# Stores issued later, activation tiles loaded two token tiles ahead, and the input layer's maxima replaced by row sums of its squares

## The chip, the core and the metric

The kernel runs on one core of a Trainium2 chip. A core has five engines that work beside each other, each through its own queue in order: TensorE (PE in the profile; PEld is its weight load), VectorE (DVE), ScalarE (ACT), GpSimd (POOL) and SyncE (SP), which here does nothing but issue transfers. Sixteen DMA engines carry the transfers. The metric is the device time of one execution, in microseconds (us), lower is better.

## The reference

Three stages follow each other: an attention whose heads are mixed before and after the softmax, a gated layer, and a layer with a squared ReLU.

```python
scores = scale * q @ k.T ; scores = mix_heads(scores, w_pre)       # 4 x 12 x 448 x 448
attn   = softmax(scores) ; attn   = mix_heads(attn, w_post)
x      = (attn @ v) laid out as 1792 tokens x 768
x      = ((x @ w1) * (x @ w2)) @ w3 @ w_out                        # 768 -> 1024 -> 1024 -> 768
h      = x @ moe2_w_in                                             # 768 -> 2048
g      = max(h, 0) ** 2
out    = g @ moe2_w_out                                            # 2048 -> 768
```

The weights of the two layers arrive as 64-bit floats. The kernel decodes them into 32-bit floats itself, and splits every factor of a product into a high and a low 16-bit half, so that a product costs three matmuls.

## The kernel before, in words

The change touches only the last third of the program, from about 832 us on: the **input layer** (`h` and `g`) and the **output layer** (`g @ moe2_w_out`).

The input layer takes the 2048 columns in eight pairs of blocks of 128 (`layer_in`). One pair is eight calls of `in_tile` (two blocks by four groups of 448 tokens), each 18 matmuls at line 1074, so 144 a pair. `in_tile` evicts a product with a ReLU on ACT (L1560), squares it in place on ACT (L1561), takes the maximum of each row of the product on DVE (`gm`, L1562), and issues a store of the square to a DRAM tensor `g` on SP (L1563). After the fourth and the eighth pair `g_scale` reduces `gm` to one number per partition (`gx`) and `send` carries it through DRAM to all partitions (`across`, then `ac`, L828 and L831, both on POOL's queue). From it comes the power of two by which `g` is scaled into 16 bits.

Beside the matmuls a stream of steps prepares weights: a chunk of 768 KB is loaded on SP into one of two `raw` buffers (L747), decoded by two ACT and four DVE operations (L797 to L811, tiles `zt` and `xa`), and either sent for a common scale and cast (`tot`, `across`, `ac`, `ws`, `w`, L889 and L892: the input weights) or stored as `kept_out` (L967: the output weights). Each raw buffer is loaded again as soon as its decode is over. A second stream, `mixed_out`, loads the kept output weights again (`ob`), adds and subtracts their quarters on POOL (`ot`, L1495) and casts the seven combinations (`ow`, L1527 and L1530): the output layer is done by a scheme that needs seven quarter products in the place of eight.

The output layer takes the tokens in 14 tiles (128 rows of either half), the first seven against the first half of the 2048 columns (partial sums stored to `acc`), the last seven against the second half (`acc` loaded again as `al`, results stored to `out`). One token tile is seven `multiply` calls of 12 matmuls (L1662), 84 in all. For it the stream `mixed_tokens` loads four quarters of `g` (`gt`, 256 KB each, L1586), forms four sums on POOL (L1594, `ss` and `gt`), and casts seven combinations to 16 bits on ACT (high half, L1615) and DVE (low half, L1616) into `ao`. `take` evicts a product: on ACT (L1676) where nothing is added, on DVE (L1678) where something is.

What sets the order: a planner in the program's own text. `now` is a planned clock that `tick` moves on, `busy` a planned load of ACT, DVE and POOL, and each stream emits its next step when its engine's planned load is less than `ahead` us in front of the clock. A transfer is written into SP's queue at the place where the program calls for it; SP then stands until that transfer's source or buffer is ready, and everything behind it stands too.

Of the kernel before, what the change touches and what calls it, by code (L numbers as in the profile page):

```python
# [10 lines left out]
F32 = mybir.dt.float32  # L11
# [7 lines left out]
P = 128  # L19
# [16 lines left out]
def talking_heads_attention_moe_moe2(  # L36
# [749 lines left out]
    def decode(raw, n, total=None, x=None, zt=None):  # L786

        lo, hi = (raw.rearrange("p (f two) -> p f two", two=2)[:, :, w] for w in (0, 1))
        z = hi.bitcast(F32)
        if x is None:  # L790
            x = pools["w"].tile([P, DM], F32, tag="xa", name="xa", bufs=3)[:, :n]
        xi = x.bitcast(I32)
        if zt is None:
            zt = pools["w"].tile([P, DM], F32, tag="zt", name="zt", bufs=1)[:, :n]
        r = n / DM
        return x, [
            (ACT, 0.9 * r, lambda: nc.scalar.activation(zt, z, AF.Abs)),  # L797
            (DVE, 1.0 * r, lambda: nc.vector.tensor_scalar(
                xi, lo, 29, 0x40000000, op0=ALU.logical_shift_right, op1=ALU.bitwise_or
            )),  # L800
            (REST, HAND, None),
            (DVE, 0.6 * r, lambda: nc.vector.tensor_scalar(
                zt, zt, F64_LEAST, F64_MOST, op0=ALU.max, op1=ALU.min
            )),
            (DVE, 1.0 * r, lambda: nc.vector.scalar_tensor_tensor(  # L805
                xi, zt.bitcast(I32), 3, xi, op0=ALU.logical_shift_left, op1=ALU.bitwise_xor
            )),
            (REST, HAND, None),
            (ACT, 1.0 * r, lambda: nc.scalar.activation(x, x, AF.Abs, accum_out=total)),  # L809
            (REST, HAND, None),  # L810
            (DVE, 1.0 * r, lambda: nc.vector.scalar_tensor_tensor(  # L811
                xi, hi, -(2 ** 31), xi, op0=ALU.bitwise_and, op1=ALU.bitwise_or
            )),
        ]
# [3 lines left out]
    def w_tile(ring, name="w"):  # L818
        return pools["w"].tile([P, 2, DM], F16, tag="wv"[ring], name=name, bufs=WB)
# [128 lines left out]
    def one_steps(i):  # L948
        kind, j = chunks[i]
        load_to(i + 1)  # L950
        t = wraw.pop(i)
        if kind == "wl":
            load_to(i + 2)
            hh = wo_tiles(j)[0]
            yield ACT, 0.9, lambda: nc.scalar.copy(hh, t.bitcast(F32))

            def low():
                nc.vector.tensor_tensor(t, t.bitcast(F32), hh, op=ALU.subtract)
                wsp["wo", j] = wsp[chunks[i]] = (hh, t)

            yield DVE, 1.0, low
            return
        n = 4 * P if kind == "w3" else DM
        if kind == "out":
            x, ops = decode(t, n, out_sums[j // OG][:, j % OG : j % OG + 1])
            yield from read_raw(i, x, ops)
            yield POOL, 0, lambda: nc.sync.dma_start(kept_out[j], x)  # L967
            if j % OG == OG - 1:
                streams.append(mixed_out(j // OG))
            return  # L970
        x, ops = (decode_alone if kind == "w3" else decode)(t, n)
        yield from read_raw(i, x, ops)
        if kind == "w3":
            hh, ll = (
                pools["w"].tile([P, 4 * P], F32R, tag="wv"[z], name="w3", bufs=WB) for z in range(2)
            )
        elif j >= NFC // 2:
            yield POOL, 0, lambda: nc.sync.dma_start(kept[j], x)
            return
        else:  # L980
            hh, ll = wo_tiles(j)
        yield ACT, 0.9 * n / DM, lambda: nc.scalar.copy(hh, x)

        def low():
            nc.gpsimd.tensor_tensor(ll, x, hh, op=ALU.subtract)
            wsp[kind, j] = (hh, ll)

        yield POOL, 2.0, low
# [54 lines left out]
    allow, ahead = [1], [4.0]  # L1043
    weights = Stream(weight_steps(2))

    def tick(us, act=0.0, dve=0.0):
        now[0] += us
        for e, c in ((ACT, act), (DVE, dve)):
            busy[e] = max(busy[e], now[0] - us) + c
        for st in streams + [weights]:  # L1050
            r = True
            while r:
                r = st.step()
            if r is None and st in streams:
                streams.remove(st)
# [29 lines left out]
    def toks(i):  # L1085
        return slice(i * S, (i + 1) * S)
# [389 lines left out]
    def mixed_out(g):  # L1476
# [10 lines left out]

        def sides(q):
            bs = [w_tile(1, "ob").rearrange("p a d -> p (a d)").bitcast(F32) for _ in range(2)]
            for z in range(2):  # L1490
                nc.sync.dma_start(bs[z], kept_out[g * OG + 2 * q + z])
            box["b"] = bs
# [44 lines left out]
    def layer_in(p, gm):  # L1537
        ws = [need(("in", 2 * p + j)) for j in range(2)]
        for st in x2_done[: B - 1]:
            finish(st)  # L1540
        sc = [sm.tile([P, B], F32, tag=f"sci{j}", name="sci") for j in range(2)]
        n = B if p else B - 1
        for j in range(2):
            nc.vector.tensor_scalar(sc[j][:, :n], kx[:, :n], ws[j][1], None, op0=ALU.mult)
        for j, i in [(j, i) for j in range(2) for i in range(n)]:
            in_tile(gm, 2 * p + j, i, ws[j][0], sc[j])
        if n < B:
            finish(x2_done[n])
            for j in range(2):
                nc.vector.tensor_scalar(sc[j][:, n:], kx[:, n:], ws[j][1], None, op0=ALU.mult)  # L1550
                in_tile(gm, 2 * p + j, n, ws[j][0], sc[j])
        for j in range(2):
            jj = (2 * p + j) % OG
            nc.vector.tensor_tensor(gm[:, jj], gm[:, jj], sc[j], op=ALU.mult)

    def in_tile(gm, jj, i, w, sc):
        pt = mm()
        product(pt, [(two(w), cols_of(c), x2[c]) for c in range(NDC)], toks(i))
        g = stage()
        nc.scalar.activation(g, pt[:, :S], AF.Relu, scale=sc[:, i : i + 1])  # L1560
        nc.scalar.activation(g, g, AF.Square)  # L1561
        nc.vector.tensor_reduce(gm[:, jj % OG, i : i + 1], pt[:, :S], axis=AX.X, op=ALU.max)  # L1562
        nc.sync.dma_start(g_d[jj // OG][jj % OG, :, toks(i)], g)  # L1563
        tick(1.13, 1.3, 0.6)

    def g_scale(g, gm):
        gx = sm.tile([P, 1], F32, tag="gx", name="gx")
        nc.vector.tensor_reduce(gx, gm.rearrange("p a b -> p (a b)"), axis=AX.X, op=ALU.max)
        nc.vector.scalar_tensor_tensor(gx, gx, 0.0, gx, op0=ALU.max, op1=ALU.mult)
        sent = send(gx, 1, nc.gpsimd)  # L1570

        def scale():
            g_up[g], g_lo[g] = pow2(largest_sent(sent, 1), 13, "gs")

        yield REST, WAY, None
        yield DVE, 0.8, scale
# [4 lines left out]

    def quarter(n, h, odd):
        g, t = divmod(n, NTT)
        x = fin.tile([P, NQ, P], F32, tag="gt", name="gt", bufs=6)
        c = h * HT + t * P
        nc.sync.dma_start(  # L1586
            x, g_d[g][odd::2, :, c : c + P].rearrange("f p t -> p f t")
        )
        return x

    def mixed_tokens():

        def add(o, a, b, op):
            nc.gpsimd.tensor_tensor(o, a, b, op=op)  # L1594

        def flat(x):
            return x.rearrange("p f t -> p (f t)")

        for n in range(2 * NTT):
            g = n // NTT  # L1600
# [1 line left out]
                yield REST, 0.5, None  # L1602
            while g not in g_up:
                yield REST, 0.5, None
            qs = {}
            for key in ((1, 0), (1, 1), (0, 0), (0, 1)):
                yield POOL, 0, lambda: qs.update({key: flat(quarter(n, *key))})
            a21, a22, a11, a12 = (qs[key] for key in ((1, 0), (1, 1), (0, 0), (0, 1)))
            yield REST, 3.5, None

            def part(k, x):
                y = fin.tile([P, 2, NQ * P], F16, tag="ao", name="ao", bufs=11)
# [5 lines left out]
                )  # L1618
                made.add((n, k))

            ss = [fin.tile([P, NQ * P], F32, tag="ss", name="ss", bufs=3) for _ in range(3)]
            s1, s2, s3 = ss
            yield POOL, 1.35, lambda: add(s1, a21, a22, ALU.add)
            yield POOL, 1.35, lambda: add(s2, s1, a11, ALU.subtract)
            yield from part(A11, a11)
# [58 lines left out]

    def put(n, q, x):
        g, t = divmod(n, NTT)
        if g == 0:
            nc.sync.dma_start(acc_d[t][:, q], x)
        else:
            h, o = divmod(q, 2)  # L1690
            r = h * HT + t * P
            nc.sync.dma_start(out[r : r + P, o * OH : (o + 1) * OH], x)

    def old(n, q):
        return al[n][q // 2][:, (q % 2) * OH : (q % 2 + 1) * OH] if n >= NTT else None

    def load_old(n):
        if NTT <= n < 2 * NTT:
            al[n] = [w_tile(0, "al").rearrange("p a d -> p (a d)").bitcast(F32) for _ in range(2)]
            for z in range(2):  # L1700
                nc.sync.dma_start(al[n][z], acc_d[n - NTT][:, 2 * z : 2 * z + 2].rearrange("p a o -> p (a o)"))
# [53 lines left out]
        tick(0.98, 0 if late else 0.55, 1.2 if late else 0.6)  # L1755
    p3(2 * NTT - 1)
    p4(2 * NTT - 1)
    order.close()


# [66 lines left out]
```

## Time and profile before

| | us |
|---|---|
| median of three runs (lowest, highest) | 1395.68 (1394.65, 1396.42) |
| the profiled execution | 1398.41 |
| span of its trace, first to last instruction | 1396.7 |
| PE busy in the span | 1262.9 (90%) |
| DVE, ACT, POOL busy | 967.6, 755.1, 524.6 |
| mean granted PE clock | 0.960 |

The time outside of the span is 1.7 us. "Busy" of PE counts a pipelined matmul for as long as it is in flight, so 90% does not say that PE is at its peak; its idle stretches, and the number of matmuls that a stretch holds, say more. A row of a timeline has the start, the length, the engine, the line and the operation, and in brackets how long the engine stood idle before it and what ended that idle time. A row of waits has the engine and line that stood, what it stood for, the total, the count and the longest.

### The profile page before, as it was taken

How to read it: one execution, taken by the hardware profiler on the slowest of the kernel's cores; microseconds unless marked ns; L12 is line 12 of the kernel's file. 1: busy time of each engine (PE TensorE's matmuls, PEld its weight loads, DVE VectorE, ACT ScalarE, POOL GpSimd, SP SyncE). 2: the span in 40 equal slices, each digit the busy share in tenths (PEclk: the TensorE clock that was granted, in tenths of full speed). 3: DMA queues.
4: the chain of work that ended last, by engine and by line, in shares of the span. 5: the costliest groups of instructions: out<-in, count | busy, mean ns of one | idle time of the engine just before them, and what ended most of it. 6: DMA issues, size and time to landing. Idle time of an engine off the chain costs nothing. (4 is left out here: it accounts for less than half of the span.)

```text
span 1396.7 us, 26110 instructions
## 1 busy us (share of the span) xinstructions
PE 1262.9 (90%) x10022; PEld 765.0 (55%) x10022; DVE 967.6 (69%) x1841; ACT 755.1 (54%) x1438; POOL 524.6 (38%) x545
## 2 busy tenths in 40 slices
PE   8999999999999999999999999998556957886687
PEld 4667767667666555556975555544223534443344
DVE  7987997987997788774976535665666537745444
ACT  7888888888874455433444425554455535432211
POOL 4988888897872010000311000000220135533311
PEclk9999999999999999999999999999778989998989
DMA  6456556556565253442323303576556434353442
GB/s 195 131 150 162 139 140 166 136 140 164 161 180 178 58 128 80 110 139 76 123 77 77 91 5 92 171 236 140 160 163 192 122 103 145 125 154 93 134 123 79
DMA packets 130337, 183.00 MB, mean 131 GB/s; under 512 B 33348, under 2 KB 110788, under 8 KB 130212
## 3 DMA queue, kind: packets, MB, share of 16 engines
q1 hardware_dynamic: 125364, 176.41, 44.3%
q0 software_dynamic: 1712, 2.51, 1.8%
q10 hardware_dynamic: 3136, 2.40, 0.7%
q8 instruction: 79, 1.29, 0.4%
q14 instruction: 46, 0.38, 0.1%
HBM read 104.37 MB, written 38.38 MB: 102 GB/s over the span
## 5 line engine op out<-in xcount | busy, mean ns | idle before, releaser
L1074 PE MATMUL mm<-x,w 128*128 128x448 f16 x2196 | 425.6, 357 | 49.6 <-ACT w L889 48.6
L1074 PEld LDWEIGHTS <-w 128*128 128x128 f16 x2304 | 226.0, 99 | 267.9 <-ACT w L889 50.7
L1662 PE MATMUL mm<-ow,ao 128*128 128x384 f16 x1176 | 214.2, 347 | 69.6 <-DVE st L1678 35.1
L1662 PEld LDWEIGHTS <-ao 128*128 128x128 f16 x1176 | 121.1, 103 | 162.5 <-issue 95.2
L285 PE MATMUL p<-Bt,wpre_k 120*120 120x448 f32 x360 | 159.4, 560 | 4.9 <-DMA Bt<-S 4.7
L381 PEld LDWEIGHTS <-EH 120*112 120x112 f16 (+1 forms) x1440 | 124.6, 130 | 44.5 <-issue 37.1
L403 DVE TENSOR_TENSOR ATl<-o,ATh 112x480 f16<-112x480 f32 x180 | 116.1, 645 | 24.5 <-ACT ATh L397 24.0
L354 POOL TENSOR_SCALAR EH<-E,st 120x448 f16<-120x448 f32 (+1 forms) x152 | 115.6, 769 | 42.7 <-DVE st L337 30.9
L307 ACT ACTIVATE E<-p,st 120x448 f32<-120x448 f32 x180 | 116.1, 645 | 23.3 <-DVE st L299 13.6
L1616 DVE SCALAR_TENSOR_TENSOR ao<-gt,gs,ao 128x512 f16<-128x512 f32 x56 | 65.9, 1208 | 86.2 <-ACT ao L1615 86.2
L381 PE MATMUL o<-wph,EH 120*112 120x120 f16 x720 | 124.0, 219 | 1.4 <-DVE ATl L403 0.7
L397 ACT CAST ATh<-o 112x480 f16<-112x480 f32 x180 | 101.1, 562 | 42.5 <-PE o L381 37.6
L381 PE MATMUL o<-wph,EL 120*112 120x120 f16 x720 | 122.0, 216 | 0.0
L381 PE MATMUL o<-wpl,EH 120*112 120x120 f16 x720 | 122.0, 216 | 0.0
L366 POOL TENSOR_TENSOR EL<-F,EH 120x448 f16<-120x448 f32 (+1 forms) x90 | 102.9, 1143 | 34.7 <-issue 21.4
L1615 ACT ACTIVATE ao<-gt,gs 128x512 f16<-128x512 f32 x56 | 38.8, 717 | 142.2 <-DMA gt<-g 129.5
L299 DVE TENSOR_REDUCE st<-p 120x1 f32<-120x448 f32 x180 | 110.2, 613 | 1.8 <-PE p L285 1.5
L1074 PE MATMUL mm<-h,M 128*128 128x448 f16 x576 | 109.8, 353 | 0.8 <-ACT M L1249 0.6
L828 POOL DMA_DIRECT2D across<-tot x15 | 8.5, 567 | 241.0 <-ACT xa L809 241.0
L1594 POOL TENSOR_TENSOR ss<-gt 128x512 f32<-128x512 f32 x28 | 40.8, 1458 | 145.9 <-DMA gt<-g 145.9
L381 PEld LDWEIGHTS <-EL 120*112 120x112 f16 x720 | 93.6, 130 | 0.0
L809 ACT ACTIVATE xa<-xa 128x768 f32<-128x768 f32 x54 | 45.5, 842 | 88.5 <-DVE xa L805 74.9
(234 smaller groups left out, 2313.6 us busy)
## 6 DMA issues: line engine op xcount, KB each, us to landing
Bt<-S SPq DMA_DIRECT2D x176, 210.0 KB
raw<-in_moe_w_out_dram SPq DMA_DIRECT2D x24, 768.0 KB
g<-st SPq DMA_DIRECT2D x64, 224.0 KB
gt<-g SPq DMA_DIRECT2D x56, 256.0 KB
raw<-in_moe_w_in_dram SPq DMA_DIRECT2D x16, 768.0 KB
raw<-in_moe_w_dram SPq DMA_DIRECT2D x14, 768.0 KB
raw<-in_moe_w_dram SPq DMA_DIRECT2D x16, 512.0 KB
kept_out<-xa SPq DMA_DIRECT2D x16, 384.0 KB
```

The costliest lines, as they stand in the source:

```text
L285: nc.tensor.matmul(pt[: n * H, :S], wpre_k.rearrange("p t g -> p (t g)")[: n * H, : n * H], Bt.pop(u)[: n * H], start=True, stop=True,)
L299: nc.vector.tensor_reduce(nsum[u][:n, 0, j : j + 1], Pp[u][:n, :S], axis=AX.X, op=ALU.max, negate=True)
L307: nc.scalar.activation(e[:n], Pp.pop(u)[:n, :S].rearrange("p (a b) -> p a b", a=EG), AF.Exp, bias=t[:n, 0, j : j + 1], scale=1.0, accum_ou ...
L354: nc.gpsimd.tensor_scalar(seven(EH[u][:n]), Ex[u][:n], inverse(u), 1.0, op0=ALU.mult, op1=ALU.mult)
L366: nc.gpsimd.tensor_tensor(a, f, b, op=ALU.subtract)
L381: nc.tensor.matmul(pt[:CP, c * n : (c + 1) * n], a[:n, c * CP : (c + 1) * CP], w[:n, :n], start=(i == 0), stop=(i == 2),)
L397: nc.scalar.copy(ATs[s][0][:, :, :, m * NR : m * NR + nr], src)
L403: nc.vector.tensor_tensor(ATs[s][1][:, :, :, a], src, ATs[s][0][:, :, :, a], op=ALU.subtract)
L809: (ACT, 1.0 * r, lambda: nc.scalar.activation(x, x, AF.Abs, accum_out=total)),
L1074: nc.tensor.matmul(pt[:, :S], w[a][:, cs], x[z][:, sl], start=(c == 0 and i == 0), stop=(c == len(parts) - 1 and i == 2),)
L1616: yield DVE, 0.7, lambda: nc.vector.scalar_tensor_tensor(y[:, 1], x, up, y[:, 0], op0=ALU.mult, op1=ALU.subtract)
L1662: nc.tensor.matmul(pt[:, :OH], y[:, a, q * P : (q + 1) * P], ow[g, q][:, w, kb], start=(start and q == 0 and m == 0), stop=(q == NQ - 1 an ...
```

## The change

It has three parts. **Stores are written into SP's queue later.** `put_later` puts a store on a list with a time, 2 us past the planned load of the engine that makes its data; `tick` issues those whose time has come, and `flush` issues the ones that a later load, or a buffer's next use, needs. The stores of `g`, `kept_out`, `acc` and `out` go this way. **The quarters of `g` are loaded one token tile earlier.** When the sums of tile n are begun, the loads of n and of n+1 are issued; the buffers hold three tiles in the place of one and a half (eight `gt`, and for every third tile the two `raw` buffers, which are free then). The sums `ss` use the three `xa` buffers of the decoder. **The row maxima go.** Squaring on ACT also gives its row sum (`accum_out`), and this sum stands for the square of the maximum; the DVE reduction, its scaling and its squaring are gone, and the planner counts no DVE time for `in_tile`.

```diff
@@ decode
         if x is None:
+            flush_kept()
             x = pools["w"].tile([P, DM], F32, tag="xa", name="xa", bufs=3)[:, :n]
@@ one_steps
-            yield POOL, 0, lambda: nc.sync.dma_start(kept_out[j], x)
+            yield POOL, 0, lambda: put_later(DVE, ("kept", j // OG), kept_out[j], x)
@@ the planner
+    puts = []
+    def put_later(eng, key, dst, src):
+        puts.append((max(busy[eng], now[0]) + 2.0, key, dst, src))
+    def flush(key=None, until=None):
+        for x in list(puts):
+            if (key is None or x[1] == key) and (until is None or x[0] <= until):
+                nc.sync.dma_start(x[2], x[3])
+                puts.remove(x)
+    def flush_kept():
+        for g in range(2):
+            flush(("kept", g))
     def tick(us, act=0.0, dve=0.0):
+        flush(None, now[0])
@@ mixed_out, sides
+            flush(("kept", g))
@@ layer_in
-        for j in range(2):
-            jj = (2 * p + j) % OG
-            nc.vector.tensor_tensor(gm[:, jj], gm[:, jj], sc[j], op=ALU.mult)
@@ in_tile
-        nc.scalar.activation(g, g, AF.Square)
-        nc.vector.tensor_reduce(gm[:, jj % OG, i : i + 1], pt[:, :S], axis=AX.X, op=ALU.max)
-        nc.sync.dma_start(g_d[jj // OG][jj % OG, :, toks(i)], g)
-        tick(1.13, 1.3, 0.6)
+        nc.scalar.activation(
+            g, g, AF.Square, accum_out=gm[:, jj % OG, i : i + 1]
+        )
+        tick(1.13, 1.3, 0)
+        put_later(ACT, ("g", jj // OG), g_d[jj // OG][jj % OG, :, toks(i)], g)
@@ g_scale
-        nc.vector.scalar_tensor_tensor(gx, gx, 0.0, gx, op0=ALU.max, op1=ALU.mult)
@@ quarter
-        x = fin.tile([P, NQ, P], F32, tag="gt", name="gt", bufs=6)
+        if n % 3 < 2:
+            x = fin.tile([P, NQ * P], F32, tag="gt", name="gt", bufs=8)
+        else:
+            if not odd:
+                raws[h] = pools["w"].tile([P, 2 * DM], F32, tag="raw", name="gt", bufs=LOADS)
+            x = raws[h][:, odd * NQ * P : (odd + 1) * NQ * P]
@@ mixed_tokens
+    def load_tokens(n):
+        if n < 2 * NTT and n not in loaded:
+            flush(("g", n // NTT))
+            loaded[n] = {key: quarter(n, *key) for key in ((1, 0), (1, 1), (0, 0), (0, 1))}
+            loaded[n]["at"] = now[0]
-            for key in ((1, 0), (1, 1), (0, 0), (0, 1)):
-                yield POOL, 0, lambda: qs.update({key: flat(quarter(n, *key))})
-            yield REST, 3.5, None
+            yield POOL, 0, lambda: load_tokens(n)
+            yield POOL, 0, lambda: load_tokens(n + 1)
+            yield REST, lambda: max(0.0, qs["at"] + 6.0 - now[0]), None
-            ss = [fin.tile([P, NQ * P], F32, tag="ss", name="ss", bufs=3) for _ in range(3)]
+            flush_kept()
+            s1, s2, s3 = (
+                pools["w"].tile([P, DM], F32, tag="xa", name="ss", bufs=3)[:, : NQ * P]
+                for _ in range(3)
+            )
@@ put, load_old and the end
-            nc.sync.dma_start(acc_d[t][:, q], x)
+            put_later(DVE, ("acc", t), acc_d[t][:, q], x)
-            nc.sync.dma_start(out[r : r + P, o * OH : (o + 1) * OH], x)
+            put_later(DVE, "out", out[r : r + P, o * OH : (o + 1) * OH], x)
+            flush(("acc", n - NTT))
+    flush()
```

PE's instructions and their order stay as they are. Three places show what moves. First SP's queue in the middle of the output layer, before: the loads of `gt` from the second group, `g_12799`, begin with the eighth token tile; each set of four stands behind the loads of `al` for that same tile.

```order
L1688 DMA acc_12805<-st 128x384
L1701 DMA al<-acc_12800 128x768 x2
L1586 DMA gt<-g_12799 128x4x128 x4
L1688 DMA acc_12805<-st 128x384
L1688 DMA acc_12806<-st 128x384
L1688 DMA acc_12805<-st 128x384
L1688 DMA acc_12806<-st 128x384
L1701 DMA al<-acc_12801 128x768 x2
L1586 DMA gt<-g_12799 128x4x128 x4
```

The same place after the change:

```order
L1606 DMA gt<-g_12799 128x4x128 x4
L1055 DMA acc_12804<-st 128x384 x2
L1055 DMA acc_12805<-st 128x384
L1055 DMA acc_12804<-st 128x384
L1731 DMA al<-acc_12800 128x768 x2
L1606 DMA gt<-g_12799 128x4x128 x4
L1055 DMA acc_12805<-st 128x384 x2
L1055 DMA acc_12806<-st 128x384
```

The eighth tile's quarters now stand four stores and two loads earlier, and the set behind `al<-acc_12800` is that of the ninth tile. Second, DVE's queue in the input layer, before, at the cast of the sixth pair's weights (`w`) and the decode that follows it:

```order
L114 RECIPROCAL ws<-ws 128x2
L1562 TENSOR_REDUCE gm<-mm 128x1
L892 SCALAR_TENSOR_TENSOR w<-xa,ws,w 128x768 x2
L798 TENSOR_SCALAR xa<-raw 128x768
L1554 TENSOR_TENSOR gm<-gm,sci 128x4 x2
L1544 TENSOR_SCALAR sci<-kx,ws 128x4 x2
L802 TENSOR_SCALAR zt<-zt 128x768
L1530 SCALAR_TENSOR_TENSOR ow<-ot,os,ow 128x768
L1562 TENSOR_REDUCE gm<-mm 128x1
L1530 SCALAR_TENSOR_TENSOR ow<-ot,os,ow 128x768
L805 SCALAR_TENSOR_TENSOR xa<-zt,xa 128x768
L1562 TENSOR_REDUCE gm<-mm 128x1
```

The same place after the change:

```order
L114 RECIPROCAL ws<-ws 128x2
L893 SCALAR_TENSOR_TENSOR w<-xa,ws,w 128x768 x2
L799 TENSOR_SCALAR xa<-raw 128x768
L803 TENSOR_SCALAR zt<-zt 128x768
L806 SCALAR_TENSOR_TENSOR xa<-zt,xa 128x768
L1548 SCALAR_TENSOR_TENSOR ow<-ot,os,ow 128x768 x2
L1562 TENSOR_SCALAR sci<-kx,ws 128x4 x2
L812 SCALAR_TENSOR_TENSOR xa<-raw,xa 128x768
```

No instruction that reads a product of PE is left in DVE's queue there, and the decode's third step stands ahead of `ow`. Third, ACT's queue where the output layer begins, before: `st<-mm,sv` is a `take` of the first token tile, `ao` are casts for the second tile, and `ao<-ss` needs a sum from POOL.

```order
L1561 ACTIVATE st<-st 128x448
L1676 ACTIVATE st<-mm,sv 128x384
L1615 ACTIVATE ao<-gt,gs 128x512 x2
L1615 ACTIVATE ao<-ss,gs 128x512
L1676 ACTIVATE st<-mm,sv 128x384 x2
```

The same place after the change:

```order
L1576 ACTIVATE st,gm<-st 128x448
L1641 ACTIVATE ao<-gt,gs 128x512 x2
L1641 ACTIVATE ao<-ss,gs 128x512
L1705 ACTIVATE st<-mm,sv 128x384 x2
```

The first `take` of the output layer has moved behind the second tile's `ao<-ss`.

## Rows read from the trace of the kernel before

**Rows 1.** Instruction groups of PE, 820 to 1397 us: busy, mean; idle, its end
```profile
L1074 PE MATMUL mm<-x,w 128*128 128x448 f16 x1152 | 227.9, 361 | 49.6 <-ACT w L889 48.6 <-DVE w L892 0.5
L1662 PE MATMUL mm<-ow,ao 128*128 128x384 f16 x1176 | 214.2, 347 | 69.6 <-DVE st L1678 35.1 <-ACT st L1676 34.4
```
**Rows 2.** Windows: length; PE, PEld, DVE, ACT, POOL busy (count); PE clock, DMA share, GB/s
```profile
859.82:1109.35 249.53, 199.96 (x1007) 99.42 (x1005) 156.99 (x267) 136.12 (x225) 33.69 (x37) 0.90 0.59 170
1109.35:1132.03 22.68, 7.97 (x50) 4.70 (x49) 3.81 (x10) 4.42 (x7) 5.44 (x7) 0.78 0.43 71
1132.03:1263.13 131.10, 104.25 (x589) 59.49 (x589) 83.06 (x101) 60.05 (x94) 64.50 (x45) 0.94 0.42 132
1263.13:1393.10 129.97, 101.94 (x540) 56.80 (x539) 61.94 (x84) 24.92 (x37) 29.29 (x20) 0.86 0.38 113
```
**Rows 3.** Timeline of PE, 860 to 1397 us: start, length, what; idle before it, its end
```profile
859.82 54.08 PE L1074 MATMUL mm<-x,w 128*128 128x448 f16 x285
...
992.72 30.63 PE L1074 MATMUL mm<-x,w 128*128 128x448 f16 x144 [19.12 <-ACT w L889]
1039.75 29.31 PE L1074 MATMUL mm<-x,w 128*128 128x448 f16 x144 [16.41 <-ACT w L889]
1079.70 29.81 PE L1074 MATMUL mm<-x,w 128*128 128x448 f16 x144 [10.64 <-ACT w L889]
...
1132.03 15.50 PE L1662 MATMUL mm<-ow,ao 128*128 128x384 f16 x84 [14.71 <-ACT st L1676]
...
1177.84 6.01 PE L1662 MATMUL mm<-ow,ao 128*128 128x384 f16 x36 [0.30 <-DVE st L1678]
...
1306.09 15.49 PE L1662 MATMUL mm<-ow,ao 128*128 128x384 f16 x84 [5.30 <-DVE st L1678]
```
**Rows 4.** Chain that ended last, 1293 to 1306 us: start, length, what
```profile
1293.03 0.63 DVE st L1678
1293.67 0.33 SPq L1701
...
1295.12 4.60 DMA gt<-g
1299.83 0.73 ACT ao L1615
...
1304.45 1.59 DVE st L1678 x3
```
**Rows 5.** Waits of SP's queue, 850 to 1397 us: total, times, longest
```profile
SPq L1563 <- ACT st L1561: 168.7, 50, 13.4
SPq L1692 <- DVE st L1678: 96.8, 18, 8.9
...
SPq L747 <- DVE xa L811: 35.0, 21, 3.3
```
**Rows 6.** Instruction groups of DVE, 820 to 1115 us
```profile
L1562 DVE TENSOR_REDUCE gm<-mm 128x1 f32<-128x448 f32 x64 | 39.6, 621 | 55.9 <-ACT st L1560 55.9
```
**Rows 7.** Timeline of DVE, then of POOL, 925 to 1000 us
```profile
986.95 0.84 DVE L1530 SCALAR_TENSOR_TENSOR ow<-ob,os,ow 128x384 f16<-128x384 f32 x1 [7.47 <-ACT ow L1527]
...
969.80 0.55 POOL L831 DMA_DIRECT2D ac<-across  x1 [11.22 <-DMA across<-om]
970.34 0.55 POOL L828 DMA_DIRECT2D across<-tot  x1
```
**Rows 8.** Timeline of DVE, then of POOL, 1074 to 1160 us
```profile
1111.29 0.16 DVE L1569 SCALAR_TENSOR_TENSOR gx<-gx 128x1 f32<-128x1 f32 x1
...
1117.18 0.55 POOL L828 DMA_DIRECT2D across<-gx  x1
1127.57 0.55 POOL L831 DMA_DIRECT2D ac<-across  x1 [9.85 <-DMA across<-gx]
```
**Rows 9.** Instruction groups of ACT, by form, 820 to 1397 us
```profile
L809 ACT ACTIVATION_READ_ACCUMULATOR xa<-xa 128x1 f32 x26 | 4.8, 186 | 0.0
```
**Rows 10.** Transfers of 1263 to 1393 us
```profile
DMA packets 15957, 14.68 MB, mean 113 GB/s; under 512 B 912, under 2 KB 14669, under 8 KB 15949
```

More of the change, by code (lines that the diff above doesn't have):

```diff
@@ L1583, in quarter @@
         g, t = divmod(n, NTT)
-        x = fin.tile([P, NQ, P], F32, tag="gt", name="gt", bufs=6)
+        if n % 3 < 2:
[4 more added lines that the diff above has]
+            x = raws[h][:, odd * NQ * P : (odd + 1) * NQ * P]
         c = h * HT + t * P
         nc.sync.dma_start(
-            x, g_d[g][odd::2, :, c : c + P].rearrange("f p t -> p f t")
-        )
-        return x
+            x.rearrange("p (f t) -> p f t", t=P),
+            g_d[g][odd::2, :, c : c + P].rearrange("f p t -> p f t"),
+        )
+        return x
+    raws, loaded = {}, {}
+    def load_tokens(n):
[3 more added lines that the diff above has]
+            loaded[n]["at"] = now[0]
     def mixed_tokens():
@@ L1594, in add @@
             nc.gpsimd.tensor_tensor(o, a, b, op=op)
-        def flat(x):
-            return x.rearrange("p f t -> p (f t)")
         for n in range(2 * NTT):
@@ L1604, in mixed_tokens @@
                 yield REST, 0.5, None
-            qs = {}
-            for key in ((1, 0), (1, 1), (0, 0), (0, 1)):
-                yield POOL, 0, lambda: qs.update({key: flat(quarter(n, *key))})
+            yield POOL, 0, lambda: load_tokens(n)
+            yield POOL, 0, lambda: load_tokens(n + 1)
+            qs = loaded[n]
             a21, a22, a11, a12 = (qs[key] for key in ((1, 0), (1, 1), (0, 0), (0, 1)))
-            yield REST, 3.5, None
+            yield REST, lambda: max(0.0, qs["at"] + 6.0 - now[0]), None
             def part(k, x):
@@ L1619, in part @@
                 made.add((n, k))
-            ss = [fin.tile([P, NQ * P], F32, tag="ss", name="ss", bufs=3) for _ in range(3)]
-            s1, s2, s3 = ss
+            flush_kept()
[3 more added lines that the diff above has]
+            )
             yield POOL, 1.35, lambda: add(s1, a21, a22, ALU.add)
@@ L1686, in put @@
         g, t = divmod(n, NTT)
+        h, o = divmod(q, 2)
+        r = h * HT + t * P
         if g == 0:
-            nc.sync.dma_start(acc_d[t][:, q], x)
+            put_later(DVE, ("acc", t), acc_d[t][:, q], x)
         else:
-            h, o = divmod(q, 2)
-            r = h * HT + t * P
-            nc.sync.dma_start(out[r : r + P, o * OH : (o + 1) * OH], x)
+            put_later(DVE, "out", out[r : r + P, o * OH : (o + 1) * OH], x)
     def old(n, q):
```

## The prediction

> **What bounds the kernel now.** I read the groups of PE first, then windows over the stages, PE's timeline, and last the chain and the waits of SP. PE's order and work do not change, so only its idle time and its clock can. In the last 535 us it stands 49.6 us in the input layer, nearly all for ACT's cast of the next pair's weights, and 69.6 us in the output layer, for evictions on DVE and on ACT [rows 1]. What it would need without standing: 285 matmuls in a row take 54.08 us, 0.190 each, so 144 (a pair) take 27.3 us; 36 of the output layer take 6.01 us, 0.167 each, so 84 (a token tile) take 14.0 us [rows 3].
>
> In the input layer the standing falls on the last three pairs: 19.12, 16.41 and 10.64 us; each then takes 29.3 to 30.6 us in the place of 27.3 [rows 3]. The window's mean granted clock is 0.90, so part of it ran at the lower of the two levels, 1.2 in the place of 2.4 GHz, and the long runs come right behind the waits [rows 2, 3].
>
> The output layer falls into three stretches [rows 2]: a start of 22.7 us with 48 matmuls and 14.71 us of idle [rows 3]; a first half of 131.1 us, 588 matmuls or seven tiles, 18.7 us each; and a second half of 130.0 us, 540 matmuls or 6.43 tiles, 20.2 each. No engine fills these halves: DVE, the busiest beside PE, has 83.06 us in 131.1 and 61.94 in 130.0, the DMA share is 0.42 and 0.38. It is a chain of latencies, and the rows of the chain name it: an eviction on DVE ends, SP gets past the load of `al`, the quarters of `g` take 4.60 us to arrive, ACT casts, DVE casts, and only then come three evictions that PE stands for [rows 4]. The eviction is late because casts of the next tile stand ahead of it in DVE's queue and wait for those quarters.
>
> **The change part by part.**
>
> *Loads a tile earlier.* The quarters of a tile are now asked for one tile (14 us or more) before the casts begin. The chain from 1293.67 to 1299.83, 6.2 us [rows 4], was paid in each tile and falls away; with it the clock, since 84 matmuls behind a wait of 5.30 us take 15.49 and not 14.0 us [rows 3]. What is late next is PE itself, then DVE. In the second half DVE's work is 61.94 / 6.43 = 9.6 us a tile [rows 2], below 14.0. One eviction has only 12 matmuls (2.0 us) to hide in, and DVE may be inside casts then, so I add 1.0 us: 15.0 a tile. Gain 6.43 x (20.2 - 15.0) = 33 us. Bounds: 14.0 a tile (40 us) and 16.5, the old 20.2 less half of the 6.2 and the clock's rest (24 us).
>
> In the first half DVE has 83.06 / 7 = 11.9 us a tile, POOL 64.50 / 7 = 9.2, ACT 8.6 [rows 2], and the mixing of weights stands in all three queues between the casts. No row shows how these interlock once the quarters are there. Bounds: 14.4 and 17.4 us a tile; I take 15.7, nearer to PE's 14.0 than to today's 18.7, since each engine has over 2 us to spare. Gain 7 x 3.0 = 21 us (9 to 30).
>
> *Stores later.* SP stood 168.7 us in front of stores of `g` and 96.8 in front of stores of `out` [rows 5]. But of the 24 weight loads between them, 21 waited at the head of the queue for their own buffer (`xa` L811, 35.0 us), so no store held them; in the input layer I give the delay nothing. In the output layer it is what lets the loads pass; that is in the sum above. Every `gt` load still stands behind two loads of `al` that wait for an eviction some 24 matmuls (4 us) into a tile, which now leaves 10 us for the 4.60 us of arrival. The stores' staging buffers are 16 against four stores a tile, so that stores which go 2 to 4 us later hold nobody.
>
> *Maxima gone.* 64 reductions of 0.621 us, 39.6 us of DVE, and 55.9 us in which DVE stood in front of one for a product of PE [rows 6]: 11.9 us of DVE's queue a pair, in the midst of the decode. ACT pays a read of the accumulator instead, 64 x 0.186 = 12 us [rows 9], 1.5 a pair, on an engine busy 136 of 250 us [rows 2]; it lies beside the matmuls. Not all of the 11.9 is on the path to the weights: the path is also made of the loads, and of the trip through DRAM. Two other causes stay: POOL stands 11.22 us for `om` before it sends `tot`, and DVE stands 7.47 us for `ow` before it reads what came back [rows 7]; the order of both is as it was. I count half, 6 us for each of the three late pairs: 18 us. Bounds: a loss of 4.5 (ACT's 1.5 a pair, were it all on the path), and a gain of 40 (nearly all of the 46 us of idle, and the clock).
>
> *Start of the output layer.* `gx` is ready at 1111.45 but POOL sends it at 1117.18, behind `om`, and stands 9.85 us for it [rows 8]. Now the last decode stands four tiles before the layer's end and not two, so `om` is through and `gx` goes 5 to 6 us earlier. But the first evictions now stand behind `ao<-ss`, which needs POOL after that wait: 24 matmuls (4.0 us) that ran before the wait come behind it. I take 2 us gained; bounds 6 gained and 8 lost (the 24 at half the clock, and `gx` no earlier).
>
> *Shared buffers.* `ss` now takes the decoder's `xa`. In the last pair sums and decode wait for each other's buffers; the first tile's sums are needed 10 us or more later, which covers a store's landing. Without that cover it is one landing, 5 us, inside the bounds of the start.
>
> Sum: 33 + 21 + 18 + 2 = 74 us from a span of 1396.7 us: 1322.7, and 1324.4 with the 1.7 us around it. The profiled execution (1398.41) stands 2.7 above the median (1395.68), so the forecast is 1395.7 - 74 = **1322 us**.
>
> **The rivals.**
>
> *More is won.* With DVE's queue free of PE the weights come a pair ahead again, as in the first pairs, where 285 matmuls run without a gap [rows 3]: input 40, start 6, halves 30 and 38: 114 us, 1282. For it: DVE's 55.9 us. Against it: the causes in rows 7 stay.
>
> *The input layer keeps its time.* If loads and the trips through DRAM are the path (the DMA share is 0.59 there, the highest of the four windows [rows 2]), 18 falls to 0 and the start may lose 8: 54 - 8 = 46 us, 1350.
>
> *DVE becomes the bound in the output layer.* Casts ran while POOL was half busy; closer together they slow each other. First half 17.4, second 16.5: 9 + 24 + 18 + 2 = 53 us, 1343.
>
> *The loads are early on paper only*: the third buffer set comes free late, so SP still stands in front of them. Then only 18 + 2 = 20 us: 1376. Against it: the set that a load needs was read a whole tile before.
>
> *Slower: transfers hold the output layer, not their order.* The second half moves 14.68 MB in 130 us [rows 10], 2.28 MB a tile; if 113 GB/s were what the queue gives under this mix, a tile would stay at 20.2 us, early loads would stand in front of `al` and push it past its tile's start, and the start's 8 us and ACT's 12 us of accumulator reads would come on top: 1416. It decides when the DMA share nears 1; it is 0.38, and 0.59 went with 170 GB/s [rows 2], which is why I give it little. The Trainium skill bears on it (DMA: Bandwidth & Descriptors, "Queues, rings and completion order"): descriptors of one ring are consumed in ring order on each DMA engine, so a load that is issued early does delay what is issued behind it. By that rule the eight loads (2 MB) now put ahead of the last weight load would delay it by some 4.6 us more than four do; the order in rows 4, where quarters behind `al` arrive together after 4.60 us, neither proves nor denies it.
>
> **How the numbers follow.** Forecast, 1300 to 1340: 0.53. More won, about 1282 to 1300: 0.14. Input unchanged, 1350: 0.12. DVE the bound, 1343: 0.12. On paper only, 1376: 0.05. Slower, 1416: 0.03; 0.01 for no change. The range leaves out the last three and a part of the second: 1288 to 1354. A measurement of this kernel tells 0.2%, 2.8 us, from none: faster 0.96, same 0.01, slower 0.03.
>
> **What would show it.** In the profile after: the `gm` reduction gone from DVE and no DVE wait for an eviction on ACT between 860 and the output layer; waits for `w` of about 13, 10 and 5 us before the last three pairs; `gt` no longer in the chain's output part, ACT's wait for it near nothing; tiles of 15 to 16 us and a granted clock above 0.95 in the second half. Wrong I am if PE still stands 5 us a tile with the quarters already landed (then DVE's queue is the bound), or if the waits for `w` stay as they are (then the path runs through transfers).

## The result and the profile after

The changed kernel takes **1337.01 us** (median of 4 runs, 1334.43 to 1338.52), the kernel before 1396.05 beside it; the ratio is 0.9575 (95% interval 0.9556 to 0.9595), so 59 us are gone. The forecast was 1322, the range 1288 to 1354. The profiled execution took 1338.06 us with a span of 1336.3, against 1398.41 and 1396.7: 60.4 us less span, and the terms below add up to this within 0.2 us.

The instruction groups of PE (busy us, mean ns of one, then idle us before them and what ended it) answer to [rows 1]:

```profile
L1091 PE MATMUL mm<-x,w 128*128 128x448 f16 x2196 | 424.2, 356 | 38.2 <-ACT w L890 37.1
L1691 PE MATMUL mm<-ow,ao 128*128 128x384 f16 x1176 | 197.6, 331 | 38.1 <-ACT st L1705 27.0
```

The first group counts more matmuls than [rows 1] does (the whole span here), but its idle time lies in the same last pairs: 49.6 us have become 38. In the output layer 69.6 have become 38.1, and of these 27.0 are one kind of wait, for an eviction on ACT. The matmuls themselves are shorter too, 331 ns in the place of 347.

Windows over the four stages, with the columns of [rows 2]:

```profile
860.00:1096.75 236.75, 198.54 (x1006) 99.25 (x1005) 120.29 (x190) 136.99 (x272) 32.99 (x36) 0.91 0.65 180
1096.75:1127.17 30.42, 4.07 (x26) 2.35 (x24) 4.24 (x9) 7.38 (x17) 5.99 (x8) 0.64 0.60 108
1127.17:1238.42 111.25, 104.67 (x612) 61.28 (x612) 98.11 (x105) 61.78 (x97) 72.08 (x48) 0.96 0.50 152
1238.42:1332.47 94.05, 88.87 (x540) 52.68 (x539) 56.28 (x80) 24.54 (x34) 22.68 (x17) 1.00 0.47 143
```

The halves shrank from 131.1 and 130.0 us to 111.3 and 94.1, and the second now runs at a granted clock of 1.00, where it had 0.86. The start grew from 22.7 to 30.4 us. PE's timeline shows both (rows of [rows 3] answer to them):

```profile
989.93 30.67 PE L1091 MATMUL mm<-x,w 128*128 128x448 f16 x144 [19.97 <-ACT w L890]
1032.39 29.93 PE L1091 MATMUL mm<-x,w 128*128 128x448 f16 x144 [11.79 <-ACT w L890]
1067.44 29.48 PE L1091 MATMUL mm<-x,w 128*128 128x448 f16 x144 [5.12 <-ACT w L890]
1096.75 4.06 PE L1691 MATMUL mm<-ow,ao 128*128 128x384 f16 x24
1127.17 28.26 PE L1691 MATMUL mm<-ow,ao 128*128 128x384 f16 x156 [26.35 <-ACT st L1705]
...
1252.93 13.81 PE L1691 MATMUL mm<-ow,ao 128*128 128x384 f16 x84 [0.70 <-DVE st L1707]
```

A tile of the second half is now 13.81 + 0.70 = 14.51 us; before, it was about 20.8 [rows 3]. And in the place of 48 matmuls and 14.71 us of idle the start has 24 and 26.35. The chain that ended last, over one tile of the second half, shows what became of [rows 4] (start, length, what):

```profile
1238.42 11.87 PE mm L1691 x72
1250.30 0.02 issue
1250.32 0.73 ACT ao L1641
1251.05 0.02 issue
1251.08 0.75 DVE ao L1642
1251.83 1.07 DVE st L1707 x2
```

No SP and no `gt` are left: the casts follow PE, not the loads.

| stretch | forecast, us | measured, us |
|---|---|---|
| second half, 540 matmuls | -33 | 130.0 to 94.1: -36 |
| first half, seven tiles | -21 | 131.1 to 107.3: -24 (111.25 less 24 matmuls, 4.0) |
| input layer | -18 | its end 1109.35 to 1096.75: -12.6 |
| start of the output layer | -2 | 22.7 to 30.4, and 24 matmuls less: **+12** |

Only the last has the wrong sign, and it lies outside its bounds of 6 gained to 8 lost. POOL's timeline shows it (start, length, what; in brackets the idle time before it and what ended it):

```profile
1071.33 1.35 POOL L1623 TENSOR_TENSOR ss<-gt 128x512 f32<-128x512 f32 x1 [11.90 <-DMA gt<-g]
1082.81 1.27 POOL L1623 TENSOR_TENSOR ss<-ss,gt 128x512 f32<-128x512 f32 x1 [10.13 <-issue]
1088.95 1.26 POOL L1623 TENSOR_TENSOR ss<-gt 128x512 f32<-128x512 f32 x1 [4.88 <-DMA kept_out<-xa]
1090.17 1.26 POOL L1623 TENSOR_TENSOR gt<-gt,ss 128x512 f32<-128x512 f32 x1
1099.13 0.56 POOL L829 DMA_DIRECT2D across<-om  x1 [7.70 <-DVE sv L1755]
1111.09 0.54 POOL L832 DMA_DIRECT2D ac<-across  x1 [11.39 <-DMA across<-om]
1111.62 0.54 POOL L829 DMA_DIRECT2D across<-gx  x1
1122.72 0.54 POOL L832 DMA_DIRECT2D ac<-across  x1 [10.55 <-DMA across<-gx]
1123.28 1.27 POOL L1623 TENSOR_TENSOR ss<-gt 128x512 f32<-128x512 f32 x1
```

Between the first and the second sum lie 10.13 us, and the third waits for a store of `xa`: the sums and the decoder want the same three buffers. Then `om` and `gx` cross DRAM one after the other, 0.5 KB each, 11.4 and 10.6 us, and POOL stands for both. Only behind them come the second tile's sums, and ACT's cast of one of these stands ahead of the first eviction, as ACT's timeline shows:

```profile
1125.93 0.72 ACT L1641 ACTIVATE ao<-ss,gs 128x512 f16<-128x512 f32 x1 [22.86 <-POOL ss L1623]
1126.56 0.56 ACT L1705 ACTIVATE st<-mm,sv 128x384 f32<-128x384 f32 x1
```

DVE's timeline shows that the last decode was held too, by the first tile's sums:

```profile
1091.47 0.56 DVE L799 TENSOR_SCALAR xa<-raw 128x768 int32<-128x768 int32 x1 [4.99 <-POOL gt L1623]
```

### The profile page after: what moved, and what is told of

Read it like the earlier page. It is cut to its first block, busy times and chain, and to the rows that moved or that the text cites. A ratio compares the mean times of both kernels' runs of the same rounds, so it can differ in the third digit from the quotient of the medians.

```text
span 1336.3 us, 26068 instructions
## 1 busy us (share of the span) xinstructions
PE 1246.2 (93%) x10022; PEld 761.2 (57%) x10022; DVE 937.3 (70%) x1759; ACT 760.6 (57%) x1502; POOL 524.7 (39%) x545
## 5 line engine op out<-in xcount | busy, mean ns | idle before, releaser
L1691 PE MATMUL mm<-ow,ao 128*128 128x384 f16 x1176 | 197.6, 331 | 38.1 <-ACT st L1705 27.0
L1691 PEld LDWEIGHTS <-ao 128*128 128x128 f16 x1176 | 116.4, 99 | 119.2 <-issue 45.5
L368 DVE SCALAR_TENSOR_TENSOR EL<-E,st,EH 120x448 f16<-120x448 f32 (+1 forms) x90 | 83.5, 928 | 11.1 <-POOL EH L354 10.7
L1091 PEld LDWEIGHTS <-M 128*128 128x128 f16 x576 | 55.9, 98 | 53.9 <-DVE M L1262 1.9
L249 ACT COPY S<-s 110x896 f32<-110x896 f32 (+1 forms) x88 | 80.4, 914 | 8.6 <-PE s L242 7.3
```

The lines of the kernel that those rows point to most:

```text
L249: nc.scalar.copy(Stile[s][:R, 2 * p : 2 * p + 2, :], Ps.pop((s, p))[:R, :, :S])
L368: nc.vector.scalar_tensor_tensor(a, e, inverse(u), b, op0=ALU.mult, op1=ALU.subtract)
L1091: nc.tensor.matmul(pt[:, :S], w[a][:, cs], x[z][:, sl], start=(c == 0 and i == 0), stop=(c == len(parts) - 1 and i == 2),)
L1691: nc.tensor.matmul(pt[:, :OH], y[:, a, q * P : (q + 1) * P], ow[g, q][:, w, kb], start=(start and q == 0 and m == 0), stop=(q == NQ - 1 an ...
```

## The experiments: the parts alone

Every time is a median of 4 runs; the ratio, with its 95% interval, is to the kernel before, run beside it (medians 1394.5 to 1396.7).

**Row sums alone.** The kernel before with this edit:

```
-        nc.scalar.activation(g, g, AF.Square)
-        nc.vector.tensor_reduce(gm[:, jj % OG, i : i + 1], pt[:, :S], ...)
+        nc.scalar.activation(g, g, AF.Square, accum_out=gm[:, jj % OG, i : i + 1])
```

> The kernel before with one part only: the input layer's 64 maxima on DVE replaced by row sums on ACT. Theory (as the prediction has it, sized by what the whole change gave to the input layer): 10 to 16 us off the waits for the weights of the last three pairs, nothing in the output layer, and a start like that of before, since the first tile's sums keep buffers of their own: 1396 - 13 = 1383 us (1376 to 1388). Rival (the row sums gave nothing, and the 12.6 us that the input layer won came from later stores and earlier loads): 1394 to 1398, with the waits of 19, 16 and 11 us as they were.

The scaling and the squaring of `gm` and DVE's planned time go with it. Measured: 1374.8 us, 0.9858 (0.9843 to 0.9873), 20 us gained and a little beyond the theory's range. The input layer ended at 1094.81, 14.5 us earlier, with waits of 16.10, 14.75 and 3.71; the first half came to 123.0 us (131.1 before), the second to 127.6. So the rival is out: row sums alone move the input layer as far as the whole change did (12.6). Some 11 us in the output layer were not foreseen; by these two traces the gain is 25.5 us and by the medians 19.7, so up to 6 of them may be the spread of single executions.

**Early loads alone.** All of the diff on `gt` and `ss`, with `put_later` issuing at once:

```
-        puts.append((max(busy[eng], now[0]) + 2.0, key, dst, src))
+        nc.sync.dma_start(dst, src)
```

> The kernel before with one part only: the quarters of g loaded one tile ahead into more buffers, and with it the sums on the decoder's shared xa buffers; every store is issued at once and the maxima stay. Theory (early loads need the late stores to pass them): about half of the output layer's 60 us, less 10 us lost in the start: 1396 - 30 + 10 = 1376 us (1365 to 1385). Rival (a whole tile of lead is cover enough, whatever stands ahead on SP): all 60 us less 10 in the start: 1346 us (1340 to 1355).

Measured: 1341.9 us, 0.9625 (0.9611 to 0.9639). The rival holds. PE's timeline has the second half at its best, and the long start too:

```profile
1103.01 4.06 PE L1694 MATMUL mm<-ow,ao 128*128 128x384 f16 x24
1133.85 20.36 PE L1694 MATMUL mm<-ow,ao 128*128 128x384 f16 x108 [26.77 <-ACT st L1708]
...
1257.19 13.81 PE L1694 MATMUL mm<-ow,ao 128*128 128x384 f16 x84 [0.70 <-DVE st L1710]
```

SP still stood 126.4 us in front of stores that waited for DVE's evictions (162.5 before: 96.8 for `out` [rows 5] and 65.7 for `acc`), and up to 21.3 us at a time, yet the loads behind them were in time (waits of SP's queue: total, times, longest; L1050 are the stores):

```profile
SPq L1050 <- DVE st L1710: 126.4, 30, 21.3
```

So the loss at the start belongs to this part, and a lead of a tile needed no help from the stores here. The input layer ended at 1103.01, 6.3 us earlier.

**Late stores alone.** `put_later` and its flushes in the kernel before.

> The kernel before with one part only: stores issued later on SP; loads, buffers and maxima as before. Theory (what bounds the output layer is the order load, cast, eviction within one tile, and the loads of al and g still stand behind the eviction): 1396 us, within 4. Rival (SP's standing of 97 us in front of stores of out is what makes the loads late): 10 to 25 us faster, 1371 to 1386, with the PE waits of the second half under 4 us a tile.

Measured: 1362.1 us, 0.9775 (0.9751 to 0.98), faster than either range. The theory is right of the second half; the rival's cause, stores that make loads late, acts in the first half alone, where the stores are those of `acc`. The input layer ended 5.2 us earlier, at 1104.15. The first half fell to 104.2 us for the same 588 matmuls (131.1 before); the second stayed at 129.7, and its chain still has the pattern of [rows 4]:

```profile
1261.23 0.63 DVE st L1697
1261.88 0.33 SPq L1721
...
1263.32 5.76 DMA gt<-g
1269.19 0.73 ACT ao L1634
```

In the first half of the kernel before, the chain reaches the quarters through a store of `acc` (L1688) in four tiles, so moving these was enough there:

```profile
1177.81 0.32 SPq L1688
...
1179.87 4.71 DMA gt<-g
```

In the second half the load of `al` (L1721) stands there, which waits for the eviction itself.

**The change without late stores.** The edit of the early loads alone, made in the kernel after.

> The kernel after without its late stores: every store is issued at once; early loads, more buffers and row sums stay. Theory (late stores are what lets the early loads pass): the output layer gives back about half of its 60 us: 1337 + 30 = 1367 us (1355 to 1375). Rival (the stores' delay is worth nothing once the loads are a tile ahead): 1337 us within 4, and the second half stays at 14.6 us a tile.

Measured: 1337.4 us, 0.9579 (0.9561 to 0.9598), the kernel after to the microsecond. The rival holds. The gains of the three parts alone are 20, 53 and 32 us, 105 in all, and together they give 59. Early loads and late stores remove the same wait of the first half: for 588 matmuls it takes 104.2 us with late stores alone, 104.8 with early loads alone, 107.3 with all three. In the input layer, too, the parts alone win 14.5, 6.3 and 5.2 us and together 12.6. Row sums add 5 us to early loads (1341.9 to 1337.4). By the end of the input layer they had won 7.4 (1103.01 to 1095.65); part of that was given back in the output layer.

## The experiments: the start of the output layer

**Own buffers** for the first tile's first two sums, in the kernel after:

```
             s1, s2, s3 = (
+                w_tile(0, "ss")....[:, : NQ * P] if n == 0 and k < 2 else
                 pools["w"].tile([P, DM], F32, tag="xa", name="ss", bufs=3)[:, : NQ * P]
-                for _ in range(3)
+                for k in range(3)
             )
```

> The kernel after, but the first tile's first two sums go into buffers of the weights' ring and no longer into the decoder's shared xa. Theory (the shared buffers hold the last decode, and with it om, gx and the start): the second sum follows the first at once, the last decode comes some 10 us earlier, om is sent before the input layer ends and gx 10 us or so earlier; PE's idle at the start of the output layer falls from 26.4 to 13 to 17 us: 1337 - 11 = 1326 us (1322 to 1331). Rival (the buffers' wait is hidden, since POOL's trips through DRAM and the evictions decide): 1337 us within 3, idle 24 us or more.

Measured: 1324.5 us, 0.9484 (0.9459 to 0.9508). The theory holds: the sums follow each other, `om` goes at 1086.94, and PE's idle time is 16.72 us.

```profile
1067.19 1.26 POOL L1623 TENSOR_TENSOR ss<-gt 128x512 f32<-128x512 f32 x1 [12.12 <-DMA gt<-g]
1068.52 1.27 POOL L1623 TENSOR_TENSOR ss<-ss,gt 128x512 f32<-128x512 f32 x1
```

**Trips in two steps.** For `om` and `gx` POOL sends the write, does other work, and sends the read later. (The expectations from here on count the pairs from nought: what they call the fifth and the sixth pair are the sixth and the seventh of the text.)

```
-            box["sent"] = send(t, 1, nc.gpsimd)
+            box["sent"] = send_parts(t, 1, nc.gpsimd)
...
+            yield REST, APART, None        # 12.0
+            yield POOL, 0, lambda: box.update(sent=box["sent"]())
             yield REST, WAY, None
```

> The kernel after, but om and gx go through DRAM in two steps: POOL sends the write, goes on with other work, and sends the read back some 12 us of the schedule later, so it stands for neither. Theory (POOL's standing for the trips is what the start and the fifth pair's weights wait for): the second tile's sums run at about 1104 us in place of 1123, PE's idle at the start falls from 26.4 to 6 to 10 us; tot of the fifth pair goes some 10 us or more earlier and its wait falls from 20.0 to 6 to 12 us: 1337 - 28 = 1309 us (1303 to 1317). Rival (the trips are slow because transfers crowd the queues, and the order on POOL is worth only the start): 1319 to 1325, with the fifth pair's wait at 17 us or more.

Measured: 1301.0 us, 0.9318 (0.9291 to 0.9345), below the theory's range. The idle time at the start is 6.70 us, the sixth pair's wait 3.22 in the place of 19.97. POOL no longer stands between the writes and the sums:

```profile
1084.67 0.56 POOL L842 DMA_DIRECT2D across<-om  x1 [7.70 <-DVE sv L1776]
1087.90 0.55 POOL L842 DMA_DIRECT2D across<-gx  x1 [2.67 <-DVE gx L1603]
1088.46 1.27 POOL L1644 TENSOR_TENSOR ss<-gt 128x512 f32<-128x512 f32 x1
```

**Both** edits together, in the kernel after.

> The kernel after with both edits, own buffers for the first tile's first two sums and the trips of om and gx in two steps. Theory (with POOL's standing gone the last decode no longer decides, so the two do not add up): like the split one or 1 to 5 us better, 1306 us (1300 to 1314). Rival (the two waits are separate and add up): 11 us better than the split one, 1298 us or less.

Measured: 1292.4 us, 0.9253 (0.9231 to 0.9275). The rival is the nearer: 8.6 us beyond the split one, against 12.5 that own buffers won by themselves. The waits are mostly separate. PE's idle time at the start is 2.78 us.

**Second tile held back** until the first tile's first two products are taken:

```
-            while n > reached[0] + 1:
+            while n > reached[0] + 1 or n == 1 and not taken:
```

> The kernel after, but the second tile's casts enter the queues only when the first tile's first two products have been taken. Theory (24 matmuls that ran before the wait now come behind it, because the second tile's cast of a sum stands ahead of the first takes on ACT): PE runs 48 or more matmuls before its long wait, the end of the wait stays, 4 us are won: 1333 us (1330 to 1336). Rival (the takes wait for something else): 24 matmuls as now, 1337 us within 2.

Measured: 1330.8 us, 0.9535 (0.9507 to 0.9562); PE ran 48 matmuls before its long wait, of 19.68 us. The theory holds, at 6 us.

**Trips in two steps in the kernel before**, without the change:

> The kernel before, with nothing of the change, but with the trips of om and gx in two steps, so that POOL stands for neither. Theory (POOL's standing is a bound of its own in the fifth pair and in the start, apart from the change): 11 us off the fifth pair's wait of 19.1, 8 to 10 us off the start: 1396 - 20 = 1376 us (1368 to 1384). Rival (the standing binds only once the change has taken away what hid it): 1390 us or more.

Measured: 1374.9 us, 0.9853 (0.9835 to 0.9871). The theory holds: the sixth pair's wait is 7.47 us (19.12 before), the start's idle 9.24 (14.71). POOL's standing was a bound of its own all along; what the change added is the wait for shared buffers ahead of it, and the 24 matmuls that now come behind it.

**Mixing entered later**, in the kernel with both edits:

```
                 yield POOL, 0, lambda: sides(q)
-                yield REST, 4.0, None
+                yield REST, 9.0, None
```

> The kernel with own buffers and two-step trips, and in it the mixing of a pair of weight tiles enters the queues 9 us of the schedule after its loads, in place of 4. Theory (the sixth pair's wait of 12.0 us is now for casts of ow that stand ahead of the cast of w on ACT and DVE and wait for ob to land, 7.75 us): its wait falls to 7 to 9 us, the rest stays: 1292 - 4 = 1288 us (1285 to 1291). Rival (the mixing only moves down the queue, into the first tile's casts): 1292 to 1300 us, with the idle time gone over to the seventh pair or to the start.

Measured: **1286.4 us**, 0.9216 (0.9202 to 0.9229), the fastest of all, 110 us below the kernel before. The theory holds: the seventh pair's wait is 4.50 us in the place of 11.99, even below its 7 to 9, the eighth's 4.66 (5.11), and nothing came back at the start:

```profile
1008.72 0.93 PE L1108 MATMUL mm<-x,w 128*128 128x448 f16 x2 [4.50 <-ACT w L907]
1010.58 28.67 PE L1108 MATMUL mm<-x,w 128*128 128x448 f16 x142 [0.93 <-DVE w L910]
...
1080.19 31.36 PE L1714 MATMUL mm<-ow,ao 128*128 128x384 f16 x192 [2.78 <-ACT st L1728]
```

**Both edits, stores at once.**

> The kernel with own buffers and two-step trips, with every store issued at once. Theory (late stores do nothing beside early loads): 1292 us within 3. Rival (with 45 us less idle time the stores come to stand in front of loads again): 1298 us or more.

Measured: 1299.9 us, 0.9315 (0.9286 to 0.9344), 7.5 above the kernel with late stores; the two intervals just do not meet. The rival's time holds, its cause is not shown. SP stands 119.1 us in front of stores that wait for DVE and 81.8 in front of stores that wait for ACT (75.3 and 12.8 with late stores), but the profiles differ by 4.0 us only, 0.7 of it at the end of the input layer and most of the rest in the first half. The profiled execution without late stores is one of the two shorter ones (1296.0 and 1296.8, the others 1302.9 and 1304.1), so what makes the remainder stays open.

## Why the forecast was right, and where it was not

**Second half and first half: right, in cause and nearly in size.** The wait for the quarters went, PE set the pace in the second half and from 1189.9 us on in the first, and the clock came back with it: 14.6 us a tile in the second half (94.05 / 6.43) against my 15.0, 15.3 in the first (107.3 / 7) against 15.7. The 1.0 us that I added for evictions was 0.70 in the second half, and the 14.0 of matmuls 13.81. The rival "on paper only" fell with these rows, and so did "transfers hold the output layer": 13.4 MB (143 GB/s for 94.05 us) moved at a DMA share of 0.47, and no tile waited for them.

The rival "DVE becomes the bound" fell as a time, 17.4 and 16.5 us a tile, but its cause shows in the first half. DVE is busy for 98.11 of the 111.25 us, the chain runs through its casts from 1153.5 to 1189.9 us, and these became longer, as the same group of DVE shows before (1132 to 1263 us) and after (1127.2 to 1238.4 us):

```profile
L1530 DVE SCALAR_TENSOR_TENSOR ow<-ot,os,ow 128x768 f16<-128x768 f32 x8 | 7.7, 1005 | 0.0
L1548 DVE SCALAR_TENSOR_TENSOR ow<-ot,os,ow 128x768 f16<-128x768 f32 x8 | 11.7, 1501 | 0.0
```

With 612 matmuls, 7.29 tiles, DVE's work is 13.5 us a tile in the place of 11.9. So of my reason for 15.7, "each engine has over 2 us to spare", DVE kept 1.8 us, and that the size came out so near is in part luck. POOL's busy share rose from 0.49 to 0.65 in this half; whether that makes the casts longer was not tried.

On the ring order that I weighed from the Trainium skill (DMA: Bandwidth & Descriptors, "Queues, rings and completion order") no run decides: the eight loads were issued from 1063.45 us on, after the last input weights (1043.56), so no pair's weights stood behind them.

**Stores later, "it is what lets the loads pass": half wrong.** With loads a tile ahead the stores' delay gave nothing (1337.4 against 1337.0); by itself it repaired the first half (131.1 to 104.2 us) and left the second alone. I had put both edits into one sum, so the total did not suffer. With the start mended the kernel with late stores was 7.5 us the faster, for a cause that stays open. In the input layer, where I gave the delay nothing, it won 5.2 us when alone.

**Input layer: right in kind, too large.** 12.6 for 18, inside my bounds; row sums alone gave 14.5, and the accumulator's reads cost what [rows 9] said (64 of 187 ns). The step that failed is "6 us for each of the three late pairs". The seventh and eighth got 4.6 and 5.5, the sixth lost 0.9, so my own sign of being wrong, a wait for `w` that stays as it was, came true for this pair. I had named the cause that stays, POOL standing for `om` before it sends `tot` [rows 7], and yet counted the sixth pair in. With the trips in two steps its wait fell to 3.22 us: there the path was POOL's queue and not DVE's. The rival "more is won" failed by the causes that I had set against it: without POOL's standing and with the mixing entered later the kernel came to 1286.4 us, near its 1282.

**Start of the output layer: wrong in sign, +12 for -2.** The step that failed is the one on shared buffers: "Without that cover it is one landing, 5 us, inside the bounds of the start". I asked whether the first tile's sums could afford to wait, and not what the wait would hold. Behind the second sum on POOL stood two more, behind these the buffer of the last decode, behind that decode `om`, and behind `om`, 11.4 us later, `gx`. So the claim that `om` "is through" before the layer's end failed: it went 2.4 us after the end. Giving the sums other buffers won 12.5 us, 9.6 of them in the start (30.4 to 20.8). That 24 matmuls would come behind the wait I had priced at 4.0 us; holding the second tile back returned 6.

Input and start together fell 19 us short of the forecast and the halves gave 6 back; that leaves 13 of the 15 us between 1322 and 1337, and the rest is spread: the two profiled executions lie 2.4 and 1.1 us above their medians.

## What to carry to other kernels

When two users come to share a ring of buffers, follow the wait into the queue of the engine that waits: price all that stands behind it there, not the one instruction that waits. An engine that sends a small transfer and then reads it back stands for the whole trip; let it do other work between the two. And parts that remove the same wait do not add up: run each alone before crediting any.

## What the runs showed of the hardware

The size of a small transfer said little on its time. In the stretch 860 to 1130 us of the kernel after, 20 writes and reads of POOL's queue went through DRAM (what, count, KB each, median us to landing):

```profile
ac<-across POOLq DMA_DIRECT2D x6, 128.0 KB, 5.8
ac<-across POOLq DMA_DIRECT2D x4, 64.0 KB, 5.7
across<-tot POOLq DMA_DIRECT2D x6, 1.0 KB, 5.7
across<-gx POOLq DMA_DIRECT2D x2, 0.5 KB, 11.6
across<-om POOLq DMA_DIRECT2D x2, 0.5 KB, 11.0
```

A write of 0.5 KB (four of them) took about twice as long as a read of 128 KB. The Trainium skill (DMA: Bandwidth & Descriptors, "Anatomy of one DMA — SWDGE (gpsimd) path") fits about 2 us plus the bytes; the medians lie at two and a half to six times that, and here the measurement decides. The two long writes at the start ran while the DMA engines were 0.90 and 0.58 busy; whether that load is the cause was not tried.
